# Outer-product decay table, two load queues and zero products at the seam of an attention and a mixture of experts

## The chip, the cores and the metric

The kernel runs on one core of one Trainium2 chip. The metric is device time in microseconds for one execution. Names of engines: TensorE (PE; PEld is its weight load), VectorE (DVE, `nc.vector`, V in the code), ScalarE (ACT, S), GpSimd (POOL, G), SyncE (SP). SP only issues transfers here.

## The reference

A linear attention with a decay per channel feeds a top-1 mixture of eight experts, and that a second dense block. Cut to what matters here:

```python
# attention: B, H, S, D = 2, 8, 768, 48
for t in range(S):
    cur = einsum('bhd,bhe->bhde', u * k[t], v[t])
    y[t] = einsum('bhd,bhde->bhe', r[t], state + cur)
    state = w * state + einsum('bhd,bhe->bhde', k[t], v[t])
# experts: 1536 tokens of 384, 8 experts, d_ff 1024
logits = x @ w_gate
expert = argmax(logits); gate_w = softmax(logits)[expert]
# token i takes the next place in its expert's list
h = relu(x_e @ w1[e]); y = gate_w * (h @ w2[e])
# second block: h = x @ w_in; solu, layer norm; @ w_out
```

`w` lies between 0.85 and 0.95, one number for each channel of each head.

## The kernel before, in words

The attention works in 12 chunks of 128 tokens (`NM = 12`, six for each of the two sequences). A chunk's decay is put into tables: `Pw` holds the powers w^(j-64) and `Qk` their counterparts, for 128 positions j; `rt` is r times `Pw`, `kt` is k times `Qk` (`prelude`), so that `scores(m)` is a product of `kt` and `rt` on TensorE (`sp`), which `mask_scores` masks into `A` on VectorE. `prelude2`, `prelude3` and `weigh` make the term of `u` (`ra`, `vab`) and the decayed keys (`kwb`); `values`, `attend`, `state` and `tokens` make the chunk's outputs `ys` and from them `xp`, the token-major rows with their gate logits.

The front of the kernel loads the decay `wcol`, then for each chunk `rkT` (r and k, channel-major, 512 KB) and `krv` (k, r, v, token-major, 576 KB; chunk 0 in two parts), and `u_sb`, a row of `u` that is read once for each of the 128 partitions, 192 KB. All loads go through SP's queue, in the order of the code. `TB` holds both tables of 130 columns. It is filled by doubling: `square(j)` makes w^(2^j) in `pf`, `invert` the reciprocals, and `extend(j)` doubles the filled part upwards on VectorE and downwards mostly on GpSimd. Chunk 0's `rt` and `kt` are made on VectorE in two halves (`fast=True`), all later ones on GpSimd in whole (128x512). `spare(n, t)` issues n products of a zero tile (`warm`, 512 columns of bf16) whose result nobody reads; 14 stand at the start, 4 ahead of `scores(0)`, 4 ahead of `scores(1)`.

The order on each engine is the order in which the code is written (a manual schedule); tiles get their waits from a framework. TensorE takes its work in that order, so an instruction that waits holds all behind it.

At the end of the attention the routing of the last chunks meets the first expert. For each chunk, `gate1` and `gate2` turn the logits of `xp` into the expert (`oh_all`), the rank of the token in the expert's list (`ranks`, a product on TensorE; `junk` reads it) and the slot; `place(i)` makes the selection matrix `P` on VectorE; `part(i)` makes `xh`, the upper part of the gated row, on ScalarE, and `other(i, xh)` makes `xl`, the rest: on GpSimd for all chunks but the last, on VectorE for chunk 11. `add(i, ...)` multiplies `xh` and `xl` by `P` into the PSUM tile `x0` (`x`, `x0` in the rows), the inputs of expert 0. Their evictions are `xhi` on ScalarE and `xlo` on VectorE; then the experts' products `hps` begin (`mm1`), with weights that ScalarE and VectorE split into `whi` and `wlo`; `hh` and `hl` evict them. `cp` counts the tokens.

Of the kernel before, what the change touches and what calls it, by code (L numbers as in the profile page):

```python
# [8 lines left out]
F32 = mybir.dt.float32  # L9
# [11 lines left out]
C = 128  # L21
# [14 lines left out]
def rwkv_moe_solu_kernel(  # L36
# [106 lines left out]
    def attention(actx):  # L143
# [12 lines left out]
        def load_chunk(m, between=None):  # L156
            a = ld.tile([128, 2, HP, C], F32, tag="rkT", name=f"rkT{m}")
            nc.sync.dma_start(out=a, in_=rkT[:, m])
            if between:
                between()  # L160
            b = ld.tile([128, 3, H, D], F32, tag="krv", name=f"krv{m}")
            chunks[m] = (a, b)
            if m:
                nc.sync.dma_start(out=b, in_=krv[:, m])
            else:
                nc.sync.dma_start(out=b[:, 0:2], in_=krv[:, m, 0:2])
# [7 lines left out]
        nc.sync.dma_start(out=u_sb, in_=u.rearrange("(o h) d -> o h d", o=1).to_broadcast([128, H, D]))  # L174
        load_chunk(1, lambda: nc.sync.dma_start(out=chunks[0][1][:, 2], in_=krv[:, 0, 2]))
# [6 lines left out]
        TB = ac.tile([128, 2, HP, 130], F32, name="TB")  # L182
        TF = TB.rearrange("p s a n -> p (s a) n")
        V.memset(TF[:, :, 64:65], 1.0)
# [8 lines left out]
        spare(WARM, wps)  # L193
        mask = ac.tile([128, 4, C], F32, name="mask")
# [4 lines left out]
        make_identity(nc, ident)  # L199

        acc0 = ac.tile([128, NE], BF16, name="acc0")
        kwb, vab = [], []
        for i in range(3):
            for lst, nm in ((kwb, "kwb"), (vab, "vab")):
                t = ac.tile([128, HP, 2, 64], F32, name=f"{nm}{i}")
                lst.append(t)
        V.memset(ones_b, 1.0)
        V.memset(acc0, 0.0)
        for i in range(3):
            for lst in (vab, kwb):  # L210
                G.memset(lst[i][:, :, :, D:64], 0.0)
# [4 lines left out]
        def square(j):  # L216
            V.tensor_tensor(pf[:, 0, :, j:j + 1], pf[:, 0, :, j - 1:j], pf[:, 0, :, j - 1:j], ALU.mult)

        def invert(a, b):
            V.reciprocal(pf[:, 1, :, a:b], pf[:, 0, :, a:b])  # L220
            G.tensor_copy(pf[:, 2, :, a:b], pf[:, 0, :, a:b])

        def extend(j):
            n = 1 << j
            up, dn = pff[:, 0:2 * HP, j:j + 1], pff[:, HP:3 * HP, j:j + 1]
            k = n if j < 6 else 1
            V.tensor_tensor(TF[:, :, 64 + n:64 + n + k], TF[:, :, 64:64 + k], up.to_broadcast([128, 2 * HP, k]), ALU.mult)
            (V if j == 5 else G).tensor_tensor(
                TF[:, :, 64 - n - k + 1:64 - n + 1], TF[:, :, 64 - k + 1:65], dn.to_broadcast([128, 2 * HP, k]), ALU.mult
            )  # L230
# [993 lines left out]
```

## Time and profile before

| what | us |
|---|---|
| median of 3 runs | 332.63 |
| lowest, highest | 332.2, 334.39 |
| the profiled execution's own time | 333.14 |
| its span, first to last instruction | 331.4 |
| TensorE busy | 315.5 (95%) |
| VectorE busy | 241.7 (73%) |
| ScalarE busy | 186.7 (56%) |
| GpSimd busy | 149.6 (45%) |
| mean granted clock of TensorE | 0.988 |

The span is that of one execution, and the execution's own time holds 1.74 us beside it. A matmul's end is modelled in the trace, so a busy TensorE also holds the time that a product takes to drain. A granted clock of 1.00 is 2.4 GHz, 0.50 is 1.2 GHz. The attention takes the first 77 us, the experts the time to about 205 us, the second block the rest.

### The profile page before, as it was taken

What the parts mean: (1) busy time and instruction counts of PE and PEld (TensorE: products, weight loads), DVE (VectorE), ACT (ScalarE), POOL (GpSimd) and SP (SyncE); (2) the same over time, 40 slices, a digit from 0 to 9 for tenths busy, and PEclk for the clock granted to TensorE, in tenths of its full rate; (3) what the DMA queues carried; (4) which work ended last, traced back from release to release, by engine and by line L of the source; (5) the groups of instructions that cost most, each with busy time, mean ns of one, the idle gap of its engine ahead of it and who ended that gap; (6) DMA issues with size and microseconds to landing.
All of it is one profiled execution on the core that took longest, in us unless ns stands there. A gap on an engine that the chain in (4) does not pass through costs nothing. (4 is left out here: it accounts for less than half of the span.)

```text
span 331.4 us, 7341 instructions
## 1 busy us (share of the span) xinstructions
PE 315.5 (95%) x2736; PEld 290.8 (88%) x2736; DVE 241.7 (73%) x556; ACT 186.7 (56%) x406; POOL 149.6 (45%) x198
## 2 busy tenths in 40 slices
PE   8899989988999999999999999999999999999990
PEld 3688878868999999999999999978999999999990
DVE  7899999957998999898999896258745555434310
ACT  1545646556749796969686867126454433444410
POOL 7889999573523232323232364414254222333321
PEclk9999999997999999999999999999999999999997
DMA  6989999444877999989898913100000000000010
GB/s 202 399 297 292 347 387 401 155 121 107 266 281 247 304 285 292 291 288 274 285 276 293 278 63 50 11 2 1 0 26 25 26 24 24 26 24 24 26 47 24
DMA packets 20395, 56.24 MB, mean 170 GB/s; under 512 B 6594, under 2 KB 9028, under 8 KB 20356
## 3 DMA queue, kind: packets, MB, share of 16 engines
q1 hardware_dynamic: 16916, 47.67, 41.0%
q0 software_dynamic: 3440, 8.06, 10.1%
q8 instruction: 23, 0.38, 0.4%
q14 instruction: 16, 0.13, 0.1%
HBM read 50.56 MB, written 5.16 MB: 168 GB/s over the span
## 5 line engine op out<-in xcount | busy, mean ns | idle before, releaser
L122 DVE TENSOR_TENSOR wlo<-raw,whi 128x768 fp32r<-128x768 f32 x57 | 52.3, 952 | 1.4 <-ACT whi L116 0.9
L804 PE MATMUL yps<-hh,wlo 128*128 128x224 f32 x192 | 52.7, 275 | 0.0
L802 PE MATMUL yps<-hh,whi 128*128 128x224 f32 x192 | 52.7, 275 | 0.0
L803 PE MATMUL yps<-hl,whi 128*128 128x224 f32 x192 | 52.6, 274 | 0.0
L116 ACT ACTIVATE whi<-raw 128x768 fp32r<-128x768 f32 x64 | 50.6, 842 | 0.0
L1044 POOL TENSOR_SCALAR e<-e,nmu 128x1024 f32<-128x1024 f32 x12 | 13.5, 1123 | 62.6 <-DVE nmu L1043 59.5
L1021 DVE TENSOR_REDUCE nm<-h 128x1 f32<-128x1024 f32 (+1 forms) x13 | 14.7, 1140 | 33.0 <-PE h L1010 30.1
L803 PEld LDWEIGHTS yps<-hl,whi 128*128 128x128 f32 x192 | 36.9, 192 | 0.0
L804 PEld LDWEIGHTS yps<-hh,wlo 128*128 128x128 f32 x192 | 36.9, 192 | 0.0
L802 PEld LDWEIGHTS yps<-hh,whi 128*128 128x128 f32 x192 | 36.9, 192 | 0.0
L120 POOL DMA_DIRECT2D wlo<-in_w x7 | 6.9, 986 | 64.6 <-ACT wlo L125 64.6
L1078 PE MATMUL o<-w_hi,shi 128*128 128x384 f32 x96 | 33.1, 345 | 0.0
L1079 PE MATMUL o<-w_lo,shi 128*128 128x384 f32 x96 | 32.2, 335 | 0.0
L1080 PE MATMUL o<-w_hi,slo 128*128 128x384 f32 x96 | 32.2, 335 | 0.0
L94 POOL DMA_INDIRECT xe<-xs,ids x16 | 20.9, 1308 | 20.5 <-PE xt L795 10.7
L816 PE MATMUL hps<-xhi,whi 128*128 128x224 f32 x192 | 28.0, 282 | 0.4 <-issue 0.4
L816 PE MATMUL hps<-xlo,whi 128*128 128x224 f32 x192 | 27.3, 278 | 0.2 <-DVE xlo L798 0.2
L822 ACT ACTIVATE hh<-hps 128x448 fp32r<-128x448 f32 x32 | 17.4, 543 | 17.7 <-PE hps L816 15.7
L816 PE MATMUL hps<-xhi,wlo 128*128 128x224 f32 x192 | 27.2, 278 | 0.0
L816 PEld LDWEIGHTS hps<-xhi,whi 128*128 128x128 f32 x192 | 24.5, 195 | 0.6 <-ACT xg L465 0.5
L816 PEld LDWEIGHTS hps<-xlo,whi 128*128 128x128 f32 x192 | 24.6, 196 | 0.4 <-DVE xlo L798 0.4
L816 PEld LDWEIGHTS hps<-xhi,wlo 128*128 128x128 f32 x192 | 24.7, 196 | 0.0
(185 smaller groups left out, 777.9 us busy)
## 6 DMA issues: line engine op xcount, KB each, us to landing
raw<-in_w SPq DMA_DIRECT2D x32, 768.0 KB
krv<-in_krv SPq DMA_DIRECT2D x11, 576.0 KB
rkT<-in_rkT SPq DMA_DIRECT2D x12, 512.0 KB
w<-in_w_in SPq DMA_DIRECT2D x8, 384.0 KB
w<-in_w_out SPq DMA_DIRECT2D x8, 384.0 KB
wlo<-in_w POOLq DMA_DIRECT2D x7, 384.0 KB
xs<-xg SPq DMA_DIRECT2D x12, 192.0 KB
krv<-in_krv SPq DMA_DIRECT2D x1, 384.0 KB
```

What stands on the lines that cost most here:

```text
L94: nc.gpsimd.indirect_dma_start(out=t[0:n, b, :], out_offset=None, in_=xs[0:rows, :], in_offset=bass.IndirectOffsetOnAxis(ap=ids[0:n, e, c: ...
L116: S.activation(hi, raw, AF.Copy)
L122: V.tensor_tensor(lo, raw, hi.bitcast(F32), ALU.subtract)
L802: T.matmul(ps, w[0][ws], x[0][xsl], start=first, stop=False, skip_group_check=True)
L803: T.matmul(ps, w[0][ws], x[1][xsl], start=False, stop=False, skip_group_check=True)
L804: T.matmul(ps, w[1][ws], x[0][xsl], start=False, stop=last, skip_group_check=True)
L816: T.matmul(ps[:, f], w1s[g][i][:, kk, wf], x[j][:, kk], start=not (i or j or f or kk), stop=j == 1 and kk == KD - 1, skip_group_check=True,)
L822: S.activation(hh, ps, AF.Relu)
L1021: V.tensor_reduce(nms[j], ps, AX.X, ALU.max, negate=True)
L1078: T.matmul(ps, hi[:, f % 4], wo[0][:, f], start=f == 0, stop=False)
L1079: T.matmul(ps, hi[:, f % 4], wo[1][:, f], start=False, stop=False)
L1080: T.matmul(ps, lo[:, f % 4], wo[0][:, f], start=False, stop=f == KF - 1)
```

## The change

The table is built from two short rows. `small_t` holds, for each table, eight fine powers (columns 0 to 7) and sixteen coarse ones in steps of eight (columns 8 to 23); `outer(t, sl)` multiplies them into 128 columns of `TB` for two of the four head pairs. `square` runs six times in a row, one reciprocal covers all powers, `down` fills the coarse row's lower half, three of its four calls on GpSimd. A `V.tensor_copy` of one column per channel goes between. Chunk 0's products follow the outer products half by half. `krv0`'s two parts and `u_sb` are issued from ScalarE's queue, the rest stays on SP's. The front half of `kt1` stays on GpSimd and the back half (`rest`) goes to VectorE behind `mask_scores(0)`. Ahead of `scores(0)` one zero product stands instead of four. At the end of the attention eleven zero products are put in at four places, and `xl` of chunk 10 is made on VectorE behind `P` of chunk 10, no longer on GpSimd.

```diff
-        def load_chunk(m, between=None):
+        def load_chunk(m):
...
-            if m:
+            if m == 0:
+                nc.scalar.dma_start(out=b[:, 0:2], in_=krv[:, m, 0:2])
+            else:
                 nc.sync.dma_start(out=b, in_=krv[:, m])
-            else:
-                nc.sync.dma_start(out=b[:, 0:2], in_=krv[:, m, 0:2])
...
-        nc.sync.dma_start(out=u_sb, in_=u.rearrange("(o h) d -> o h d", o=1).to_broadcast([128, H, D]))
-        load_chunk(1, lambda: nc.sync.dma_start(out=chunks[0][1][:, 2], in_=krv[:, 0, 2]))
+        nc.scalar.dma_start(out=u_sb, in_=u.rearrange("(o h) d -> o h d", o=1).to_broadcast([128, H, D]))
+        nc.scalar.dma_start(out=chunks[0][1][:, 2], in_=krv[:, 0, 2])
+        load_chunk(1)
...
+        small_t = ac.tile([128, 2, HP, 32], F32, name="small_t")
+        SF = small_t.rearrange("p s a n -> p (s a) n")
+        V.memset(SF[:, :, 16:17], 1.0)
+        V.memset(small_t[:, 0, :, 0:1], 1.0)
...
+        def down(eng, j, a, b):
+            eng.tensor_tensor(
+                SF[:, :, a:b], SF[:, :, 17 - (b - a):17], pff[:, HP:3 * HP, j:j + 1].to_broadcast([128, 2 * HP, b - a]),
+                ALU.mult,
+            )
+
+        G.tensor_copy(pf[:, 0, :, 0:1], wcol)
+        make_identity(nc, ident)
+        square(1, low=wcol)
+        for j in range(2, 7):
+            square(j)
+        G.tensor_copy(pf[:, 2, :, 3:7], pf[:, 0, :, 3:7])
+        V.reciprocal(pf[:, 1, :, 0:7], pf[:, 0, :, 0:7])
+        V.tensor_copy(small_t[:, 1, :, 0:1], pf[:, 1, :, 0:1])
+        ups = SF.rearrange("p q (k n) -> p q k n", k=2)
+        for j in range(3):
             n = 1 << j
+            V.tensor_tensor(
+                ups[:, :, :, n:2 * n], ups[:, :, :, 0:n],
+                pff[:, 0:2 * HP, j:j + 4:3].unsqueeze(3).to_broadcast([128, 2 * HP, 2, n]), ALU.mult,
             )
+        down(G, 3, 15, 16)
+        down(G, 4, 13, 15)
+        down(V, 5, 9, 13)
+        down(G, 6, 8, 9)
+        square(7, G)
+
+        def outer(t, sl):
+            V.tensor_tensor(
+                TB[:, t, sl].rearrange("p a (x y) -> p a x y", y=8),
+                small_t[:, t, sl, 8:24].unsqueeze(3).to_broadcast([128, 2, 16, 8]),
+                small_t[:, t, sl, 0:8].unsqueeze(2).to_broadcast([128, 2, 16, 8]), ALU.mult,
+            )
...
+            if m == 0:
+                for sl in (front, back):
+                    outer(0, sl)
+                    outer(1, sl)
+                    weighted(V, rt, tr, Pw, sl)
+                    weighted(V, kt, tk, Qk, sl)
+                return
+            weighted(G, rt, tr, Pw, whole)
+            if m > 1:
+                weighted(G, kt, tk, Qk, whole)
+                return
+            weighted(G, kt, tk, Qk, front)
+            return lambda: weighted(V, kt, tk, Qk, back)
...
-        spare(4, wps)
+        spare(1, wps)
         scores(0)
-        prelude(1)
+        rest = prelude(1)
...
         mask_scores(0)
+        rest()
         together(products)
...
-            if i < NM - 1:
+            if i < NM - 2:
                 G.tensor_tensor(xl, xgs[i], xh.bitcast(F32), ALU.subtract)
...
         m = NM - 1
+        fill = ps_1.tile([128, 512], F32, tag="ra", name="fill")
+        spare(4, fill)
         tokens(m)
...
         scatter(m - 1)
-        los[m - 1] = other(m - 1, his[m - 1])
         store(m - 1)
...
         onehots[m - 1] = place(m - 1)
+        los[m - 1] = other(m - 1, his[m - 1])
         next(steps)
...
-        for i in (m - 1, m):
-            add(i, his)
-            add(i, los)
+        spare(1, fill)
+        add(m - 1, his)
+        add(m - 1, los)
+        spare(3, fill)
+        add(m, his)
+        add(m, los)
...
+        spare(3, fill)
         V.tensor_copy(tot, cp)
```

What stands in a row on the engines. VectorE in the front, before, from the second reciprocal to the front half of chunk 0's products (`TB` is the table, `pf` the powers):

```order
L220 RECIPROCAL pf_107<-pf_107 128x4x4
L227 TENSOR_TENSOR TB_128<-TB_128,pf_107 128x8x8
L217 TENSOR_TENSOR pf_107<-pf_107 128x4
L227 TENSOR_TENSOR TB_128<-TB_128,pf_107 128x8x16
L227 TENSOR_TENSOR TB_128<-TB_128,pf_107 128x8x32
L228 TENSOR_TENSOR TB_128<-TB_128,pf_107 128x8x32
L227 TENSOR_TENSOR TB_128<-TB_128,pf_107 128x8
L262 TENSOR_TENSOR rt0_200<-rkT0_110,TB_128 128x256
L262 TENSOR_TENSOR kt0_199<-rkT0_110,TB_128 128x256
```

Each doubling needs the one before, and the products stand behind the last. The same engine there after the change, from the one reciprocal on (`small_t` holds the two short rows):

```order
L230 RECIPROCAL pf_107<-pf_107 128x4x7
L231 COPY small_t_129<-pf_107 128x4
L235 TENSOR_TENSOR small_t_129<-small_t_129,pf_107 128x16
L235 TENSOR_TENSOR small_t_129<-small_t_129,pf_107 128x16x2
L235 TENSOR_TENSOR small_t_129<-small_t_129,pf_107 128x16x4
L219 TENSOR_TENSOR small_t_129<-small_t_129,pf_107 128x8x4
L246 TENSOR_TENSOR TB_128<-small_t_129 128x256 x2
L269 TENSOR_TENSOR rt0_194<-rkT0_110,TB_128 128x256
L269 TENSOR_TENSOR kt0_193<-rkT0_110,TB_128 128x256
L246 TENSOR_TENSOR TB_128<-small_t_129 128x256 x2
```

The doubling over `TB` has gone, and the products of chunk 0's front half now stand between the outer products of the front and of the back half.

VectorE at the end of the attention, before, from the last gate to chunk 11's `xl`:

```order
L446 RECIPROCAL gate11_1454<-gs11_1430 128x1
L560 TENSOR_SCALAR P0_10_1458<-iota_w_196,t110_1379,rank_all_78 128x224
L450 SCALAR_TENSOR_TENSOR junk11_1460,rank_all_78<-xp11_1389,oh_all_77 128x8
L560 TENSOR_SCALAR P0_11_1462<-iota_w_196,t111_1432,rank_all_78 128x224
L579 SCALAR_TENSOR_TENSOR xl11_1464<-xp11_1389,gate11_1454,xh11_1456 128x384
```

Only chunk 11's `xl` is made there. The same place on VectorE after the change:

```order
L468 RECIPROCAL gate11_1453<-gs11_1431 128x1
L583 TENSOR_SCALAR P0_10_1457<-iota_w_190,t110_1375,rank_all_78 128x224
L602 SCALAR_TENSOR_TENSOR xl10_1459<-xp10_1335,gate10_1400,xh10_1402 128x384
L472 SCALAR_TENSOR_TENSOR junk11_1461,rank_all_78<-xp11_1390,oh_all_77 128x8
L583 TENSOR_SCALAR P0_11_1463<-iota_w_190,t111_1433,rank_all_78 128x224
L602 SCALAR_TENSOR_TENSOR xl11_1465<-xp11_1390,gate11_1453,xh11_1455 128x384
```

`xl10` has come in between `P0_10` and `junk11`, the rank of chunk 11.

TensorE at the end of the attention, before, from the sums of chunk 10 to the counts (`x0` is the first expert's input):

```order
L652 MATMUL x0_1403<-P0_10_1458,xh10_1401 128x224 x3
L652 MATMUL x0_1403<-P0_10_1458,xl10_1446 128x224 x3
L652 MATMUL x0_1403<-P0_11_1462,xh11_1456 128x224 x3
L652 MATMUL x0_1403<-P0_11_1462,xl11_1464 128x224 x3
L696 LDWEIGHTS ones_b_76
L696 MATMUL cp_1498<-acc9_1324,ones_b_76 128x8
```

The sums follow one another. The same place on TensorE after the change, as far as the first of the three zero products ahead of chunk 11's sums:

```order
L192 LDWEIGHTS warm_132
L192 MATMUL fill_1385<-warm_132 128x512
L677 MATMUL x0_1404<-P0_10_1457,xh10_1402 128x224 x3
L677 MATMUL x0_1404<-P0_10_1457,xl10_1459 128x224 x3
L192 LDWEIGHTS warm_132
L192 MATMUL fill_1385<-warm_132 128x512
```

One zero product (`fill`) now stands ahead of chunk 10's sums and three stand between them and chunk 11's; four more stand ahead of `tokens(11)` and three behind the counts.

## Rows read from the trace of the kernel before

**Rows 1.** Page, part 2: TensorE's granted clock in tenths, 40 slices of 8.3 us.
```profile
PEclk9999999997999999999999999999999999999997
```

**Rows 2.** Timeline of TensorE, first expert: start us, us, engine, line, operation, count.
```profile
77.03 1.69 PE L816 MATMUL hps<-xhi,whi 128*128 128x224 f32 x6 [0.38 <-issue]
...
79.80 1.33 PE L816 MATMUL hps<-xlo,whi 128*128 128x224 f32 x6
...
80.96 0.83 PE L816 MATMUL hps<-xhi,whi 128*128 128x224 f32 x6
```

**Rows 3.** Windows of 1 us: busy us by engine, then PEclk, DMA share, GB/s.
```profile
74.00:75.00 1.00, 0.19 (x2) 0.00 (x1) 0.82 (x3) 0.04 (x1) 0.98 (x2) 1.00 0.56 194
...
77.00:78.00 1.00, 0.97 (x4) 0.85 (x5) 0.50 (x2) 1.00 (x3) 0.57 (x1) 0.70 0.55 197
78.00:79.00 1.00, 1.00 (x7) 1.00 (x7) 1.00 (x6) 1.00 (x3) 0.00 (x0) 0.50 0.04 8
```

**Rows 4.** Timeline, end of the attention; in brackets idle time before, and its releaser.
```profile
70.07 1.14 PE L395 MATMUL xp<-sel,ys 112*128 112x104 f32 x8 [0.37 <-ACT ys L346]
...
73.11 0.43 DVE L560 TENSOR_SCALAR P<-iota_w,t,rank_all 128x224 fp32r<-128x224 f32 x1
...
74.25 1.01 POOL L575 TENSOR_TENSOR xl<-xg,xh 128x384 fp32r<-128x384 f32 x1
74.35 1.05 DVE L560 TENSOR_SCALAR P<-iota_w,t,rank_all 128x224 fp32r<-128x224 f32 x1
...
75.31 0.59 PE L652 MATMUL x<-P,xl 128*128 128x224 f32 x3 [1.12 <-POOL xl L575]
75.32 0.61 DVE L579 SCALAR_TENSOR_TENSOR xl<-xp,gate,xh 128x384 fp32r<-128x384 f32 x1
...
76.61 0.85 ACT L691 ACTIVATE xhi<-x 128x224 fp32r<-128x224 f32 x3
...
77.50 0.99 DVE L693 TENSOR_TENSOR xlo<-x,xhi 128x224 fp32r<-128x224 f32 x3 [1.21 <-ACT xhi L691]
...
81.86 0.62 DVE L823 SCALAR_TENSOR_TENSOR hl<-hps,hh 128x448 fp32r<-128x448 f32 x1 [0.66 <-ACT hh L822]
```

**Rows 5.** Windows: ten microseconds of the chunk loop, columns as in rows 3.
```profile
30.00:40.00 10.00, 10.00 (x160) 8.54 (x160) 9.58 (x33) 5.69 (x20) 9.12 (x11) 1.00 0.95 328
```

**Rows 6.** Timeline of the front, columns as in rows 4.
```profile
2.42 1.02 DVE L232 COPY pf<-wcol 128x4 f32<-128x4 f32 x1 [1.05 <-DMA wcol<-in_wd]
...
3.21 0.20 POOL L211 MEMSET kwb<- 128x128 f32 x1
...
3.48 0.37 DVE L217 TENSOR_TENSOR pf<-pf 128x4 f32<-128x4 f32 x2
...
3.88 0.23 DVE L220 RECIPROCAL pf<-pf 128x12 f32<-128x12 f32 x1
...
5.41 1.16 POOL L228 TENSOR_TENSOR TB<-TB,pf 128x64 f32<-128x64 f32 x3
...
5.84 1.18 PEld L191 LDWEIGHTS <-warm 128*128 128x128 bf16 x6 [0.17 <-issue]
...
6.94 0.42 DVE L262 TENSOR_TENSOR rt<-rkT,TB 128x256 f32<-128x256 f32 x1
...
7.96 0.42 DVE L262 TENSOR_TENSOR kt<-rkT,TB 128x256 f32<-128x256 f32 x1
7.97 0.09 POOL L516 MEMSET neg_half<- 128x1 f32 x1
...
10.05 1.18 POOL L262 TENSOR_TENSOR rt<-rkT,TB 128x512 f32<-128x512 f32 x1 [0.89 <-DMA rkT<-in_rkT]
...
12.23 0.57 DVE L269 TENSOR_TENSOR ra<-krv 128x384 f32<-128x384 f32 x1 [0.60 <-DMA krv<-in_krv]
...
12.42 1.16 PE L297 MATMUL sp<-rt,kt 64*128 64x128 f32 x16 [1.59 <-POOL kt L262]
```

**Rows 7.** Windows: half a microsecond of the front, columns as in rows 3.
```profile
6.00:6.50 0.50, 0.50 (x5) 0.20 (x3) 0.50 (x2) 0.00 (x0) 0.50 (x2) 1.00 0.64 145
```

More of the change, by code (lines that the diff above doesn't have):

```diff
@@ L193, in attention @@
         spare(WARM, wps)
+        kwb, vab = [], []
+        for i in range(3):
+            for lst, nm in ((kwb, "kwb"), (vab, "vab")):
+                t = ac.tile([128, HP, 2, 64], F32, name=f"{nm}{i}")
+                lst.append(t)
+                G.memset(t[:, :, :, D:64], 0.0)
         mask = ac.tile([128, 4, C], F32, name="mask")
@@ L219, in invert @@
[L219 to L223, printed above, removed]
-            n = 1 << j
[L225 to L229, printed above, removed]
-            )
@@ L232, in attention, with square @@
-        V.tensor_copy(pf[:, 0, :, 0:1], wcol)
-        square(1)
-        square(2)
-        invert(0, 3)
-        for j in range(3):
-            square(j + 3)
-            extend(j)
-        square(6)
-        invert(3, 7)
-        extend(3)
-        square(7)
-        for j in range(4, 7):
-            extend(j)
-        Pw, Qk = TB[:, 0, :, 0:C], TB[:, 1, :, 1:C + 1]
+        def square(j, eng=V, low=None):
+            low = pf[:, 0, :, j - 1:j] if low is None else low
+            eng.tensor_tensor(pf[:, 0, :, j:j + 1], low, low, ALU.mult)
@@ L246, in attention @@
+        def outer(t, sl):
[4 more added lines that the diff above has]
+            )
+        Pw, Qk = TB[:, 0], TB[:, 1]
         w128 = pf[:, 0, :, 7:8]
@@ L253, in attention, with prelude @@
         rts, kts, avs = {}, {}, {}
-        def prelude(m, fast=False):
+        def prelude(m):
             tr, tk = chunks[m][0][:, 0], chunks[m][0][:, 1]
@@ L259, in prelude, with weighted @@
             kts[m], rts[m] = kt, rt
-            for sl in (slice(0, 2), slice(2, 4)) if fast else (slice(0, 4),):
-                for o, i, t in ((rt, tr, Pw), (kt, tk, Qk)):
-                    (V if fast else G).tensor_tensor(o[:, sl], i[:, sl], t[:, sl], ALU.mult)
+            def weighted(eng, o, i, t, sl):
+                eng.tensor_tensor(o[:, sl], i[:, sl], t[:, sl], ALU.mult)
+            front, back, whole = slice(0, 2), slice(2, 4), slice(0, 4)
+            if m == 0:
[11 more added lines that the diff above has]
+            return lambda: weighted(V, kt, tk, Qk, back)
         def prelude2(m):
@@ L492, in scatter @@
             scattered.append(ins)
-        prelude(0, fast=True)
+        prelude(0)
         gate_on = ac.tile([128, 1], F32, name="gate_on")
```

17 lines of the change are left out of this document (1 added, 16 removed).

## The prediction

> **What bounds the kernel now.** I read the page's slices first, then TensorE's products and the windows where the clock dips, then the chain in front of that place, then the start. The granted clock of TensorE is full except in two slices near a quarter of the span [rows 1]. There the first expert's products begin: the first 18 (three groups of six) take from 77.03 to 80.96, while the six that follow need 0.83 us [rows 2]. The clock is the cause: 0.70, then 0.50 of 2.4 GHz, so from about 77.4 until that faster group it stands at the 1.2 GHz level [rows 3]. Before it fell, TensorE had been busy for only 0.19 us of the microsecond from 74 [rows 3]: it waited 1.12 us for `xl` of chunk 10, which GpSimd wrote until 75.26 [rows 4]. Behind 81 us the experts follow one another on TensorE, so what this place loses the end loses, unless VectorE becomes late. In the chunk loop TensorE is busy 10.00 us of 10 [rows 5], so the loop, too, starts and ends earlier by what its first wait loses: TensorE stands idle 1.59 us before `scores(1)` at 12.42, until GpSimd has made `kt1` [rows 6]. Two places can pay: before 12.42, and from 74 to 81.
>
> **The end of the attention.** Eleven zero products come in there, and each costs 0.20 us (six in 1.18 us) [rows 6].
> The four ahead of `tokens(11)` take 0.80 us where TensorE was idle 0.37 us for `ys` [rows 4], so the chain behind (gate, ranks, place) starts 0.43 us later.
> Against that, `xl` of chunk 10 leaves GpSimd. VectorE's `P` of chunk 11 lasted 1.05 us and ended at 75.40, just after GpSimd's 1.01 us ended at 75.26, where `P` of chunk 10 took 0.43 us [rows 4]; I price it at 0.43 again. The chain then reads: `P` of chunk 10 ends at 73.54 + 0.43 = 73.97; `xl` of chunk 10, now on VectorE, takes 0.61 us as its twin for chunk 11 does [rows 4], until 74.58; the two small operations of the ranks that stood between the rows of `P` take some 0.25 us; `P` of chunk 11 lasts until 75.26 and `xl` of chunk 11 until 75.87. Before, that was 75.32 + 0.61 = 75.93. So the order gains 0.06 us, as good as nothing: what the move gives, the four products take. ScalarE's `xg` and the last adds follow as before, and the evictions `xhi` start at some 76.5 instead of 76.61. The one product and the three between the adds lie where TensorE waits for `xl` and `P`, which covers them; without that wait they would cost 0.8 us.
> The three products behind the counts take 0.60 us and end near 77.1; TensorE would have waited for the third `xhi` until 77.4 anyway (0.85 us from 76.5) [rows 4]. That wait covers them; without it they would cost 0.6 us.
> If the clock stays at 2.4 GHz, the last four of the first six products start at 77.4 and end at 77.9, the next six at 78.8, `xlo` has been ready since 78.4 [rows 4], and the third six end at 79.6. The next group stood at 80.96 [rows 2]: a gain of 1.36 us.
> What is late next is VectorE. It splits weights there almost without a pause, and has little but its idle 0.66 us before `hl` of the first product group [rows 4] and the 0.1 us of the earlier start to give: 0.8 us. TensorE meets it again where the second expert's `xlo` is made. The term is therefore -0.8 to -1.36 us; I take the middle, **-1.1**. Its other bound is 0, if the clock falls all the same.
>
> **The front.** The last `kt0` half ends at 8.38 [rows 6]. The new VectorE chain, from `wcol` at 2.42: six dependent squares at 0.19 us each (two took 0.37), 3.55; a reciprocal of 0.23, 3.8; a copy of four elements, 0.1; four short products, priced as the squares, 4.7; two outer products, priced as the `rt0` row of the same 256 elements, at the 0.34 us that lie between such rows (three of them from 6.94 to 7.96) [rows 6], 5.4; then `rt0` and `kt0` if `rkT0` is there, 6.1; and the same again for the back half, 7.5. That is 0.9 us earlier than 8.38. ScalarE's scaled copies and `QN` follow the table, off the path.
> But `scores(1)` waits for `kt1`, and that for the landing of `rkT1`: GpSimd had been idle 0.89 us when `rkT1` released it at 10.05, and its two products of 1.18 us end at 12.4 [rows 6]. The table alone thus gives nothing here. What gives is the split of `kt1`: GpSimd's second 1.18 us becomes half of one, 0.59 us, and VectorE makes the other half (0.42 us) behind `mask_scores(0)`, about 9.9 to 10.4, beside GpSimd. So -0.59 us at the same landing. Queued behind VectorE's half, which now waits for `rkT1`, are the reduction and `vab0`; `values(0)` needs them only after `scores(1)`, so they hold nobody. The second limit is `krv1`: VectorE waited for it until 12.23, its product takes 0.57 us, and `A` of chunk 1 can follow no sooner than 12.8 [rows 6], while `scores(1)` would now end at 13.0; so little more than -0.6 is to be had unless `krv1`, too, lands earlier. The three zero products that go (0.60 us) lay where TensorE waited for `kt0`.
> The landing itself is the unknown. Ahead of `rkT1` the one queue carries `rkT0`, `krv0`'s first part and `u_sb`; with two queues `rkT1` is second on its own but shares the engines with all of ScalarE's 0.79 MB. The DMA engines moved 145 GB/s where `u_sb`'s broadcast rows run [rows 7], against 328 in the loop [rows 5]. If the second queue brings `u_sb`'s 0.2 MB to that rate, all behind it lands 0.8 us earlier, and the front's best bound is -1.4. If the queues merely share, 0.2 MB more come ahead of `rkT1`, 0.6 us at 328 GB/s, and nothing is left. I take the landing as unchanged, nearer to the row as it is: **-0.6**.
> A rule speaks against the second queue. The Trainium skill, "DMA: Bandwidth & Descriptors", section "Issuing engines are not separate DMA queues", says that transfers of different issuing engines run on the same 16 DMA engines and interleave, so that a second issuer saves only the time of issuing. No run here shows two issuers yet. By it the front gives nothing.
>
> **The sum.** The profiled execution took 333.14 us, 1.74 us more than its span: 333.14 - 1.1 - 0.6 = 331.4. It lay 0.5 us over the median of the runs, 332.63, so against that I forecast **330.9**.
>
> **The rivals.** (1) *The queues only share*: 0 in place of -0.6, 331.5. For it speaks that TensorE's first wait ends with a landing; against it the 145 GB/s, which leave room.
> (2) *The four-element copy is held*. In the trace such a copy lasted 1.02 us and ended at 3.44, just after GpSimd's run of memsets at 3.41 [rows 6]; `P` of chunk 11 shows the same [rows 4]. The new copy is released by the same reciprocal as GpSimd's three short products (1.16 us for three in the old table), behind which its square, iotas and a cast are queued without a wait (from the products' end at 6.57 to 8.06, 1.5 us) [rows 6]. If GpSimd comes first, the copy ends 2.7 us late, near 6.5, the table is whole at 9.3, `A` of chunk 0 ends near 12.2, `vab0` near 13.7, after `scores(1)`, and the loop starts some 0.5 us later than before: 332.0. Against it: the copy is short, and one instruction of GpSimd stands no longer than some 0.4 us.
> The Trainium skill agrees: "GPSIMD Engine Reference", section "1. Specifications", has GpSimd's way into SBUF shared with VectorE, with contention when VectorE works in a 2-port mode; the 1.02 us row bears it out.
> (3) *The clock falls all the same*, behind the zero products: the end term is gone, 332.0. Against it: they put 1.4 us of work where TensorE idled most.
> (4) *Slower: the fall comes ahead of the zero products.* TensorE takes its work in order, and six zero products stand ahead of its last adds and of the first expert. At 1.2 GHz they take 0.40 us each, +1.2, and the six adds 1.33 instead of 0.83 [rows 2], +0.5; with the front's -0.6 and the order's -0.1 that is +1.0, 333.6. It decides by when the clock falls: before about 75, rather than at 77.4. For it: the chain now starts 0.43 us later, so TensorE still idles between the adds; against it: four products fill the time right before.
>
> **How the numbers follow.** Both places pay: 0.50. Rival 1: 0.18; rival 2: 0.15; rival 3: 0.08; rival 4: 0.06; the rest is unnamed. Low end: both best bounds, -1.4 and -1.36, from 332.63, 329.9, less 0.5 for the spread of the runs: 329.4. High end: rival 2 or 3 with the same spread, 332.5. One per cent, about what a measurement of this kernel can tell from no change, is 3.3 us; both best bounds make 2.8. So faster by more 0.08, within 0.89, slower 0.03.
>
> **What would show it.** The first expert's products in groups of 0.83 us from the second group on, and a clock of 1.00 from 74 to 82; `P` of chunk 11 at 0.4 us; `kt1` in two halves that overlap, `scores(1)` near 11.8; VectorE's copy at 0.1 us. The forecast fails if `rkT1` lands elsewhere than near 10 us, if TensorE's idle time near 10 us lowers the clock in the chunk loop, or if VectorE eats the gain between 81 and 95 us.

## The result, and the profile after

The changed kernel takes 336.35 us (median of four runs, 336.06 to 337.2), the kernel before 332.89 in the same comparison (four runs, 332.2 to 334.39): a ratio of 1.0111, 95% interval 1.0079 to 1.0143. It is slower by about 1%, where 330.9 was forecast. The profiled execution took 336.44 us with a span of 334.7, against 333.14 and 331.4: 3.3 us more.

Two marks divide the span: the start of `scores(11)`, the last chunk's, and the first expert's fourth group of six products, the first that ran at full speed before [rows 2]. From the start to `scores(11)` the kernel before takes 62.28 us and the changed one 65.42 (+3.14). From there to the fourth group it is 18.68 against 16.91 (-1.77), and from the fourth group to the end 250.44 against 252.37 (+1.93). So the front or the loop loses, the end of the attention wins as it was meant to, and something behind it takes that win back. These are two single profiles; how far such marks move from one profile to the next is said under the table of experiments.

The page's slices of the granted clock show the first two of these. The dip near a quarter of the span [rows 1] is gone, and a new one stands in the second slice:

```profile
PEclk9799999999999999999999999999999999999997
```

**The front.** VectorE's rows of the changed kernel (start, duration, operation, and in brackets the idle time ahead and what ended it):

```profile
3.62 0.17 DVE L216 TENSOR_TENSOR pf<-wcol 128x4 f32<-128x4 f32 x1 [2.21 <-DMA wcol<-in_wd]
...
5.26 0.17 DVE L231 COPY small_t<-pf 128x4 f32<-128x4 f32 x1
...
6.36 0.76 DVE L246 TENSOR_TENSOR TB<-small_t 128x256 f32<-128x256 f32 x2
7.97 0.42 DVE L269 TENSOR_TENSOR rt<-rkT,TB 128x256 f32<-128x256 f32 x1 [0.84 <-DMA rkT<-in_rkT]
```

`wcol` comes 1.2 us later than the 2.42 of [rows 6], and when the front half of the table is ready, VectorE waits again, for `rkT0`; before, its `rt0` row of 6.94 waited for no landing. `rkT0` is issued at 1.23 and is there 6.7 us later; on one queue (b_split and a_nosplit below) it lands 4.2 us after its issue. GpSimd, behind that:

```profile
10.67 0.19 POOL L540 COPY held<-gate_on 128x1 f32<-128x1 f32 x1 [3.08 <-DVE gate_on L521]
10.81 1.27 POOL L269 TENSOR_TENSOR rt<-rkT,TB 128x512 f32<-128x512 f32 x1
```

This is one way by which a late front reaches the loop (the other is VectorE's own queue, see a_spare below): in both kernels GpSimd's work on chunk 1 stands behind `held`, a copy of `gate_on`, and VectorE writes `gate_on` behind chunk 0's products, here at 10.54. `rkT1` holds nobody: it landed near 9.8 us (8.1 us after its issue at 1.70). Before, the copy was done by 9.2 and it was the landing of `rkT1` that released GpSimd, at 10.05 [rows 6]. TensorE, in the same stretch:

```profile
1.31 6.05 PE L192 MATMUL wps<-warm 128*128 128x512 bf16 x15 [1.31 <-DVE warm L187]
8.78 0.71 PE L319 MATMUL sp<-rt,kt 64*128 64x128 f32 x8 [1.42 <-DVE kt L269]
10.12 1.23 PE L319 MATMUL sp<-rt,kt 64*128 64x128 f32 x8 [0.62 <-DVE kt L269]
...
12.19 1.69 PE L192 MATMUL wps<-warm 128*128 128x512 bf16 x4
13.81 1.16 PE L319 MATMUL sp<-rt,kt 64*128 64x128 f32 x16
```

The two halves of `scores(0)` are eight products of the same shape each, but 0.71 us becomes 1.23, and four zero products take 1.69. The second half and what follows run at the lower level of the clock, by the window's granted clock (columns: busy time and instructions of PE, PEld, DVE, ACT and POOL, then clock, DMA share, GB/s):

```profile
10.00:15.00 5.00, 4.88 (x33) 3.29 (x34) 4.68 (x9) 1.65 (x7) 4.04 (x5) 0.66 1.05 396
```

`scores(1)` starts at 13.81 instead of 12.42 [rows 6]. From `scores(2)` to `scores(11)` the loop takes 46.22 us (19.20 to 65.42) against 45.06 before, and there GpSimd's products have become slower than the 1.18 us of [rows 6] (grouped by line, 14 to 70 us; total, mean ns):

```profile
L269 POOL TENSOR_TENSOR rt<-rkT,TB 128x512 f32<-128x512 f32 x10 | 13.1, 1306 | 0.0
L269 POOL TENSOR_TENSOR kt<-rkT,TB 128x512 f32<-128x512 f32 x10 | 13.0, 1301 | 0.0
```

**The end of the attention.** The first expert's groups stand 0.67 to 0.74 us apart from the first on, where [rows 2] has groups of 1.3 to 1.7 us. The first of them comes no sooner behind `scores(11)` than before (14.83 us against 14.75); the whole gain lies between the groups:

```profile
80.25 0.90 PE L845 MATMUL hps<-xhi,whi 128*128 128x224 f32 x6
80.99 0.83 PE L845 MATMUL hps<-xhi,wlo 128*128 128x224 f32 x6
81.66 0.83 PE L845 MATMUL hps<-xlo,whi 128*128 128x224 f32 x6
82.33 0.83 PE L845 MATMUL hps<-xhi,whi 128*128 128x224 f32 x6
```

**Behind it.** VectorE's rows from 87 us: three of them, each 0.2 to 0.6 us long elsewhere, take about 3 us and end together near 91.18:

```profile
87.57 0.35 DVE L910 TENSOR_SCALAR da<-w 128x384 int32<-128x384 int32 x1
87.84 3.34 DVE L761 TENSOR_SCALAR cnt<-tot 128x8 f32<-128x8 f32 x1
87.96 3.22 DVE L912 SCALAR_TENSOR_TENSOR da<-w,da 128x384 int32<-128x384 int32 x1
88.44 2.75 DVE L763 TENSOR_SCALAR cnt<-tot 128x8 f32<-128x8 f32 x1
91.24 0.56 DVE L914 CUSTOM_DVE_ANT_0 da<-w,da 128x768 uint16<-128x768 uint16 x1
```

At the same time GpSimd makes the descriptors of the second expert's gather and then eight memsets without a pause; the last ends at 91.15:

```profile
85.36 1.82 POOL L94 DMA_INDIRECT xe<-xs,ids  x1 [5.03 <-DMA ids<-idx]
87.49 1.02 POOL L94 DMA_INDIRECT xe<-xs,ids  x1 [0.31 <-issue]
88.52 0.49 POOL L952 MEMSET yThi<- 128x448 f32 x1
...
90.85 0.30 POOL L952 MEMSET yTlo<- 128x224 f32 x1
```

TensorE pays for it ten microseconds later (weight load row):

```profile
100.71 0.74 PEld L845 LDWEIGHTS hps<-xlo,whi 128*128 128x128 f32 x6 [1.73 <-DVE xlo L827]
```

In the kernel before, the same memsets ran from 84.42 to 87.06, and only one row, `da` at 86.28 with 1.00 us instead of 0.35, was held, until just behind their end. They moved because the gather waits for `ids`, not for TensorE: it starts 4.05 us later (85.36 against 81.31), while TensorE's fourth group and VectorE's decoding come only some 1.3 us later. Of the 4.05 us, 2.78 are the later scatter of the ids, and 1.27 the longer way from the scatter to the gather (6.00 us against 4.73). The second part isn't the change's doing: b_split below, which leaves this place as it was, has 6.00 us too, and a long hold.

### The profile page after: what moved, and what is told of

The parts are those of the page before. It is cut to its first block, busy times and chain, and to the rows that moved or that the text cites. A ratio compares the mean times of both kernels' runs of the same rounds, so it can differ in the third digit from the quotient of the medians.

```text
span 334.7 us, 7358 instructions
## 1 busy us (share of the span) xinstructions
PE 317.3 (95%) x2744; PEld 290.7 (87%) x2744; DVE 246.6 (74%) x557; ACT 186.8 (56%) x406; POOL 149.1 (45%) x195
## 5 line engine op out<-in xcount | busy, mean ns | idle before, releaser
L845 PE MATMUL hps<-xhi,whi 128*128 128x224 f32 x192 | 27.1, 277 | 0.1
L845 PEld LDWEIGHTS hps<-xhi,wlo 128*128 128x128 f32 x192 | 24.0, 192 | 0.0
```

The costliest lines, as they stand in the source:

```text
L845: T.matmul(ps[:, f], w1s[g][i][:, kk, wf], x[j][:, kk], start=not (i or j or f or kk), stop=j == 1 and kk == KD - 1, skip_group_check=True,)
```

## The experiments

**Theory.** Three costs that the prediction had left out make the loss: the second queue delays the loads on which the front waits; GpSimd's products are slower with rows of 128 elements in the table; and GpSimd's memsets hold VectorE. **Rivals:** the clock in the front is the whole of the front's loss; VectorE has too much work behind 82 us. Every kernel's ratio is to the kernel before, run beside it.

| kernel | ratio, 95% interval | `scores(11)` | to the fourth group | to the end |
|---|---|---|---|---|
| before | 1 | 62.28 | 18.68 | 250.44 |
| changed | 1.0111 (1.0079 to 1.0143) | 65.42 | 16.91 | 252.37 |
| a_oneq | 1.0045 (1.0025 to 1.0065) | 63.08 | 17.46 | 252.46 |
| a_spare | 1.0097 (1.0071 to 1.0123) | 65.22 | 17.43 | 252.45 |
| a_tb130 | 1.0079 (1.0049 to 1.0109) | 64.46 | 17.26 | 252.28 |
| a_mem | 1.0079 (1.0049 to 1.0110) | 65.39 | 17.47 | 251.24 |
| b_tail | 0.9996 (0.9967 to 1.0024) | 61.57 | 17.07 | 252.46 |
| b_tailclear | 0.9936 (0.9913 to 0.9959) | 61.86 | 17.34 | 250.00 |
| b_split | 0.9996 (0.9970 to 1.0021) | 61.94 | 18.25 | 252.31 |
| a_best1 | 0.9958 (0.9936 to 0.9981) | 62.02 | 17.39 | 249.89 |
| b_clear | 0.9970 (0.9938 to 1.0003) | 62.10 | 20.45 | 249.95 |
| b_fillclear | 0.9941 (0.9921 to 0.9962) | 61.60 | 17.59 | 250.01 |
| a_wcol | 1.0164 (1.0126 to 1.0201) | 66.34 | 16.42 | 252.44 |
| a_nosplit | 0.9927 (0.9900 to 0.9954) | 62.11 | 17.42 | 250.07 |
| a_gateq | 1.0154 (1.0126 to 1.0183) | 69.47 | 17.29 | 252.34 |
| a_pad | one run, 335.98 us | 64.35 | 17.49 | 252.46 |

The three columns on the right are the three parts of each profiled span. They vary from one execution to the next, too: over the five traces whose front is that of the kernel before (before, b_tail, b_tailclear, b_clear, b_fillclear), `scores(1)` starts between 11.70 and 12.42 and `scores(11)` between 61.57 and 62.28.

**One queue (a_oneq).**

```diff
-            nc.scalar.dma_start(out=b[:, 0:2], in_=krv[:, m, 0:2])   # m == 0
+            nc.sync.dma_start(out=b[:, 0:2], in_=krv[:, m, 0:2])
-nc.scalar.dma_start(out=u_sb, ...)
-nc.scalar.dma_start(out=chunks[0][1][:, 2], in_=krv[:, 0, 2])
-load_chunk(1)
+nc.sync.dma_start(out=u_sb, ...)
+load_chunk(1, lambda: nc.sync.dma_start(out=chunks[0][1][:, 2], in_=krv[:, 0, 2]))
```

> The changed kernel with all of the front's loads back on SyncE's queue, in the order of the kernel before. If the second queue is what made the front late: wcol lands near 2.4 us instead of 3.62, rkT0 before 7 instead of 7.97, scores(0) starts about 1.1 us earlier, scores(1) near 12.7 instead of 13.81; the rest of the loop and the end keep their losses, so 335.0 us against 336.35 for the changed kernel. If the queue costs nothing on the path and the clock near 10 us is the whole of the front's loss (the rival): wcol may land early, but scores(1) stays at 13.4 or later, 336.2 us.

Measured: `wcol` is there again at 2.50 (VectorE's rows), `rt0` starts at 6.26 without a wait, `scores(0)` at 7.07, `scores(1)` at 11.22, earlier than in any trace of the old front; the clock stays at 1.00 in the windows to 68 us.

```profile
2.50 0.40 DVE L217 TENSOR_TENSOR pf<-wcol 128x4 f32<-128x4 f32 x1 [1.09 <-DMA wcol<-in_wd]
...
6.26 0.42 DVE L270 TENSOR_TENSOR rt<-rkT,TB 128x256 f32<-128x256 f32 x1
```

The ratio falls from 1.0111 to 1.0045, 0.66% or 2.2 us; `scores(11)` comes 2.34 us sooner. The second queue is the largest of the costs found. That its loads hinder each other by sharing the DMA engines fits `rkT0`'s 6.7 us against 4.2, but no run shows how they do it.

**Three zero products back ahead of `scores(0)` (a_spare).**

```diff
-        spare(1, wps)
+        spare(4, wps)
         scores(0)
```

> The changed kernel with the three zero products put back ahead of scores(0). If TensorE's idle 1.42 us before scores(0) is what lowers the clock from 10 to 15 us: the granted clock of that window goes from 0.66 to about 0.9 or more, the back half of scores(0), the four transposes and the four zero products ahead of scores(1) take 1.5 us less, scores(1) starts near 12.9, 335.2 us. If the clock falls for the later idle time of 0.62 us, or falls all the same (the rival): the clock stays near 0.66 and the time at 336.3 us.

The clock does stay up, as expected (window of this kernel):

```profile
10.00:15.00 5.00, 4.16 (x42) 2.96 (x44) 4.93 (x8) 1.56 (x7) 4.43 (x5) 1.00 1.06 400
```

and `scores(1)` starts at 12.73 instead of 13.81. But `scores(2)` comes at 18.95 against 19.20, `scores(11)` at 65.22 against 65.42, and the ratio, 1.0097, is not to be told from 1.0111. TensorE's rows of a_spare:

```profile
1.31 5.94 PE L192 MATMUL wps<-warm 128*128 128x512 bf16 x18 [1.31 <-DVE warm L187]
8.69 0.71 PE L319 MATMUL sp<-rt,kt 64*128 64x128 f32 x8 [1.44 <-DVE kt L269]
...
14.17 0.62 PE L339 MATMUL yp<-ident,vab 128*112 128x128 f32 x4 [0.27 <-DVE vab L307]
...
18.40 0.62 PE L339 MATMUL yp<-ident,vab 128*112 128x128 f32 x4 [1.08 <-DVE vab L307]
```

The three products didn't shorten the idle time that was under suspicion: it is 1.44 us, as long as the 1.42 without them, because the 18 zero products took no longer than the 15 of the changed kernel. So the idle time by itself doesn't lower the clock. The five traces with the changed front and one zero product (changed, a_tb130, a_mem, a_pad, a_wcol) all show 0.66 or 0.67 in this window, this one shows 1.00; that the three products make the difference is likely, but it rests on one trace. The price is clear: behind `scores(1)` TensorE waits here for `vab0` and `vab1`, the end of VectorE's chain, which the clock of TensorE doesn't touch, and GpSimd's first product of chunk 1 starts at 10.72 here and at 10.81 there. So the clock is not the front's loss.

**Rows of 130 elements (a_tb130), and with both tables at column 0 (a_pad).**

```diff
-        TB = ac.tile([128, 2, HP, C], F32, name="TB")
+        TB = ac.tile([128, 2, HP, 130], F32, name="TB")
-        Pw, Qk = TB[:, 0], TB[:, 1]
+        Pw, Qk = TB[:, 0, :, 0:C], TB[:, 1, :, 1:C + 1]     # a_tb130
+        Pw, Qk = TB[:, 0, :, 0:C], TB[:, 1, :, 0:C]         # a_pad
```

> The changed kernel with the tables of powers in rows of 130 elements, the keys' table starting at column 1, as in the kernel before; everything else as changed. If the narrower rows made GpSimd's products slow: its rt and kt rows in the loop go back from 1.30 to 1.18 us, the loop loses 1.1 us less between scores(2) and scores(11), 335.2 us. If they are slow for another reason (the place of other tiles, VectorE's work beside them): the rows stay at 1.30 us and the time at 336.3 us.

> The changed kernel with the tables in rows of 130 elements, both starting at column 0. If the length of the rows is what counts: rt and kt on GpSimd at 1.18 to 1.22 us. If the column at which the keys' table starts counts: kt stays at 1.30 us and rt with it.

GpSimd's rows in a_pad (those of a_tb130 read 1221 and 1217):

```profile
L269 POOL TENSOR_TENSOR rt<-rkT,TB 128x512 f32<-128x512 f32 x10 | 12.2, 1222 | 0.0
L269 POOL TENSOR_TENSOR kt<-rkT,TB 128x512 f32<-128x512 f32 x10 | 12.2, 1215 | 0.0
```

From `scores(2)` to `scores(11)` both take 45.26 us, as against 46.22 of the changed kernel; every kernel with rows of 130 needs 45.06 to 45.46, every one with rows of 128 46.22 to 46.88. So the length of the rows counts and the column doesn't: 1.0 us. One rival is left: a longer table also moves the tiles behind it, by 64 bytes in each partition, and no run separates this from the length. The single ratio, 1.0079, agrees, but alone would not tell a_tb130 from the changed kernel's 1.0111.

**The memsets ahead of the gather: four of them (a_mem), or all eight (b_tailclear, b_clear and others below).** Four were moved in a_mem, not eight as its expectation says; the other four belong to the next expert and are issued right behind the gather.

```diff
+        clear(0)              # the four memsets of yT of expert 1
+        clear(1)              # the four of expert 2; not in a_mem
         xraw = load_xe(1, 0, 2)
...
```

> The changed kernel with the eight memsets of the output rows put ahead of the second expert's gather on GpSimd, so that they run while it waits for the ids. If these memsets and the gather hold VectorE from 87.9 to 91.2: the two rows of cnt go from 3.34 and 2.76 to 0.17 us, da from 3.22 to 0.56, TensorE's wait of 1.5 us for xlo goes, and with it 1.9 us: 334.4 us. If VectorE is late there because it has too much to do, as the prediction's bound had it (the rival): the rows get short, but TensorE waits as before, 336.0 us or more.

The held row shrinks with the memsets that are left, and ends again with the last of them (VectorE, then GpSimd, of a_mem):

```profile
88.37 2.06 DVE L761 TENSOR_SCALAR cnt<-tot 128x8 f32<-128x8 f32 x1
88.49 1.94 DVE L912 SCALAR_TENSOR_TENSOR da<-w,da 128x384 int32<-128x384 int32 x1
```

```profile
88.03 1.01 POOL L94 DMA_INDIRECT xe<-xs,ids  x1 [0.31 <-issue]
89.05 0.49 POOL L943 MEMSET yThi<- 128x448 f32 x1
...
90.10 0.30 POOL L943 MEMSET yTlo<- 128x224 f32 x1
```

The last part of the span falls from 252.37 to 251.24 us, and TensorE's longest wait for `xlo` from 1.5 to 0.9 us; the ratio, 1.0079, is not to be told from 1.0111. The theory's size was half right because the edit was half of it.

**The end of the attention alone, on the kernel before (b_tail), and with the eight memsets ahead (b_tailclear).** b_tail is the diff of the change from `other` on and nothing else.

> The kernel before with the change's end of the attention alone: the eleven zero products, and xl of chunk 10 on VectorE. If the prediction's end term is right: no clock fall near 78, the fourth group of six products (80.96 us) 1.4 to 1.9 us earlier, and 0.8 to 1.4 us off the time of the kernel before. If the gain is given back because the second expert's gather, and the memsets behind it on GpSimd, come later against TensorE's work and hold VectorE's integer and count rows for some 3 us instead of 0.6 (my theory): the products are as early, but the time is within 0.4 us of the kernel before, and rows of cnt or da of 2 to 3.3 us stand between 85 and 90.

> The same, with the eight memsets of the output rows put ahead of the second expert's gather. If they are what holds VectorE: the held rows shrink to what the gather itself takes (1.0 us or less), and the time is 1.0 to 1.8 us below the kernel before. If the gain is lost elsewhere behind 82 us (VectorE's own work, the landing of the ids, the gather): no more than 0.5 us below it.

b_tail shows both halves of my theory. The fourth group comes 17.07 us after `scores(11)` instead of 18.68, no window is below 1.00 to 100 us, and the time is the kernel before's: 0.9996. VectorE and GpSimd in b_tail:

```profile
84.22 3.34 DVE L738 TENSOR_SCALAR cnt<-tot 128x8 f32<-128x8 f32 x1
84.33 3.22 DVE L889 SCALAR_TENSOR_TENSOR da<-w,da 128x384 int32<-128x384 int32 x1
```

```profile
84.89 0.48 POOL L929 MEMSET yThi<- 128x448 f32 x1
...
87.22 0.30 POOL L929 MEMSET yTlo<- 128x224 f32 x1
```

With the memsets ahead, from 77.19 to 80.84, the same rows are short, TensorE is busy 10.00 us of each 10 from 80 to 100, and 0.9936 is 2.1 us below the kernel before:

```profile
84.78 0.17 DVE L738 TENSOR_SCALAR cnt<-tot 128x8 f32<-128x8 f32 x1
84.90 0.56 DVE L889 SCALAR_TENSOR_TENSOR da<-w,da 128x384 int32<-128x384 int32 x1
```

The rival falls: VectorE has the same work in both, and keeps up once it isn't held. The gather by itself holds nothing: its second part runs from 84.38 to 85.45, right beside these short rows.

**The memsets alone (b_clear).**

> The kernel before with nothing but the eight memsets put ahead of the second expert's gather. In its profile they held VectorE for 0.64 us only, so by that row alone it should be within 0.3 us of the kernel before. If other executions of the kernel before have the long hold too (the profile of the kernel with the split alone had one of 3.0 us), it is 0.5 to 1.5 us faster, and the tail's own gain is the rest of the 2.1 us.

0.9970, with an interval that just takes in 1; the second expectation is the nearer one. The last part is 249.95 us, half a microsecond below the kernel before's profile and 2.4 below the traces with the long hold. That profile's short hold was thus one of two that occur: b_split has a long one. The zero products' own gain is what lies between b_clear and b_tailclear, 0.34% or 1.1 us; the two intervals overlap. The single executions tell more: of b_clear's twelve, four took 330.08 to 330.62 us at a mean granted clock of 0.992 to 0.994, as b_tailclear's eight did (329.85 to 330.99, 0.992 to 0.995), and four, the profiled one among them, 333.78 to 334.25 at 0.979 to 0.983. So without the zero products the clock's loss differs from one execution to the next, and what they buy is that it stays small in all.

**Zero products without the move of `xl` (b_fillclear).** The diff of b_tailclear without the three places of `xl`.

> The kernel before with the eleven zero products and the memsets ahead of the gather, but with xl of chunk 10 on GpSimd and in its old place. By the prediction's step the zero products keep the clock up and the move gives back what the four ahead of the last tokens take (0.43 us): no clock fall, 0.3 to 0.5 us slower than with the move, so about 1.7 us below the kernel before. If the clock falls all the same while TensorE waits for that xl (the rival): the first groups take 1.3 to 1.7 us again, and it is less than 1.2 us below.

0.9941 against 0.9936: no difference. The clock stays up, and the expected loss of 0.3 to 0.5 us isn't seen. In this execution `P` of chunk 11 took 0.53 us beside GpSimd, not the 1.05 of [rows 4].

**Half of the second `kt` on VectorE, alone on the kernel before (b_split).**

```diff
-        prelude(1)
+        prelude(1, late=late)      # G: rt whole, kt[:, 0:2]
         mask_scores(0)
+        late.pop()()               # V: kt[:, 2:4] = tk * Qk
```

> The kernel before with half of the second chunk's k on VectorE alone. If the prediction's term is right: scores(1) 0.6 us earlier at the same landing of rkT1, scores(11) and the end 0.5 to 0.6 us earlier. If the chunk loop takes it back because GpSimd's chain, not scores(1), sets the pace (the rival): scores(1) near 11.8, scores(2) within 0.2 us of 17.2, the time within 0.2 us of the kernel before.

0.9996. `scores(1)` starts at 11.66, but the traces with the unsplit front have 11.70 to 12.42. The two engines stand in each other's way: VectorE's half runs beside GpSimd's `rt1` (9.61 to 10.79) and then beside GpSimd's half (VectorE, then GpSimd):

```profile
9.92 1.15 DVE L265 TENSOR_TENSOR kt<-rkT,TB 128x256 f32<-128x256 f32 x1
```

```profile
10.75 0.86 POOL L264 TENSOR_TENSOR kt<-rkT,TB 128x256 f32<-128x256 f32 x1
```

instead of 0.42 and 0.59 us. From GpSimd's first product of chunk 1 at 9.61 to `scores(1)` it is 2.05 us, against 2.37 unsplit [rows 6]: 0.3 us, which the loop doesn't pass on (5.13 us from `scores(3)` to `scores(4)` here, 4.96 before).

**The three costs taken out together (a_best1), and that without the split (a_nosplit).** One queue, rows of 130, the eight memsets ahead; in a_nosplit `kt1` is GpSimd's alone.

> The changed kernel with the three suspected costs taken out together: the front's loads on one queue, the tables in rows of 130, the eight memsets ahead of the gather. If the queue, GpSimd's slower products and the held VectorE are the whole loss: scores(11) near 61.9, the fourth group of six near 79.6, no held row over 1.1 us, and 2.0 to 2.6 us below the kernel before. If they are not (the rival): within 1 us of the kernel before.

> One queue, tables in rows of 130 and memsets ahead of the gather, as in the run with the three costs taken out, but with the whole kt of the second chunk on GpSimd: of the change's front only the outer products are left. If the split is worth its 0.59 us: 0.4 to 0.6 us slower than that run, so some 0.9 us below the kernel before. If VectorE's half and GpSimd's hinder each other so that the split gives nothing (0.94 us for VectorE's half in that run, 0.42 expected): scores(1) within 0.3 us of 11.5, and 1.2 to 2.0 us below the kernel before.

The marks of a_best1 came as expected (62.02, 79.41, no held row); the ratio, 0.9958, is 1.4 us below the kernel before, less than the 2.0 to 2.6 expected, though its span is 2.1 below. a_nosplit gives 0.9927, 2.4 us below; `scores(1)` at 12.12 is later than my 11.5. The split gains nothing in either comparison. Beside a_nosplit, a_best1 starts `scores(1)` 0.93 us earlier, `scores(2)` 0.34 and `scores(11)` 0.09: between the first two TensorE waits twice for `vab`, which stands behind the half of `kt1` in VectorE's queue (TensorE's rows of a_best1; in a_nosplit neither waits):

```profile
12.63 0.62 PE L340 MATMUL yp<-ident,vab 128*112 128x128 f32 x4 [0.28 <-DVE vab L308]
...
16.02 0.62 PE L340 MATMUL yp<-ident,vab 128*112 128x128 f32 x4 [0.24 <-DVE vab L308]
```

The kernel a_nosplit is the fastest measured, 1.8% below the changed one (0.9927 / 1.0111), though not to be told from b_tailclear: the outer products, by themselves, leave the time as it was.

**What a second queue does (a_wcol, a_gateq).**

```diff
-nc.sync.dma_start(out=wcol, in_=wd)                   # a_wcol
+nc.scalar.dma_start(out=wcol, in_=wd)                 # a_wcol: first on ScalarE's queue
+V.tensor_copy(chunks[0][1][:, 0, 0, 0:1], wcol[:, 0]) # a_gateq: ScalarE's three loads wait for it
```

> The changed kernel with wcol's load moved ahead of the others on ScalarE's queue, so that no large load is issued before or beside it. If the late wcol (3.62 us) alone makes the front late: it lands near 2.5, scores(0) starts near 7.2, the clock stays up, and the time falls by 2 us against the changed kernel, to 0.45 per cent over the kernel before. If rkT0, which shares the engines with 0.6 MB of the other queue, sets the pace as well (my theory): scores(0) no sooner than 8.2, and no more than 0.7 us is won.

> The changed kernel with ScalarE's three loads held until wcol has landed (one more small copy on VectorE, 0.2 us). If wcol's lateness is the cost of the second queue: wcol lands near 2.5, scores(0) starts near 7.4, the clock stays up, and the time is that of the kernel with one queue, 0.3 to 0.6 per cent over the kernel before. If the large loads of two queues hinder each other as well (the rival): rkT0 lands after 7.2, scores(0) starts at 8.2 or later, 0.8 per cent or more over it.

Both came out slower than the changed kernel. a_gateq's rival had that sign, but not its reason: `rkT0` is in time there. In a_wcol the small load, though first in its queue, landed at 4.97 (VectorE's row), while `rkT0` was issued beside it at 0.80 on the other queue, against what its expectation says; `scores(0)` starts at 9.21, and `rt0` doesn't wait for `rkT0`:

```profile
4.97 0.17 DVE L216 TENSOR_TENSOR pf<-wcol 128x4 f32<-128x4 f32 x1 [3.56 <-DMA wcol<-in_wd]
```

In a_gateq `wcol` lands in time and `scores(0)` starts at 7.07, as that theory said, but now ScalarE's loads, issued from 2.63 behind SyncE's, come late: `krv0`, `u_sb`, and last the part of `krv0` that `vab0` needs (VectorE):

```profile
9.11 0.57 DVE L291 TENSOR_TENSOR ra<-krv 128x384 f32<-128x384 f32 x1 [0.76 <-DMA krv<-in_krv]
...
10.81 0.57 DVE L293 TENSOR_TENSOR ra<-ra,u_sb 128x384 f32<-128x384 f32 x1 [1.07 <-DMA u_sb<-in_u]
...
15.42 0.56 DVE L307 TENSOR_TENSOR vab<-krv,ra 128x384 f32<-128x384 f32 x1 [1.81 <-DMA krv<-in_krv]
```

`scores(2)` then starts at 22.65. So it is neither `wcol` alone nor `rkT0` alone: one queue's order is the order in which the front needs its loads, and with two queues some load that is needed early runs beside or behind one that isn't.

## Why the prediction was wrong, point by point

- **"The clock fall ... avoided"**: right. The mark of the end term, from `scores(11)` to the fourth group, is 16.4 to 17.6 us in the thirteen traces with zero products and 18.25 to 20.45 in the three without. The term of -0.8 to -1.36 was -1.77 in this profile: the working gave each group 0.83 us, a row that holds the end of its last product too, and the groups stand 0.67 to 0.74 us apart. That the order of the operations would gain as good as nothing was right as well (14.83 us to the first group, 14.75 before).
- **"What is late next is VectorE"**: the engine and the place were right (`xlo` of the second expert), the reason and the size weren't. I took VectorE's own work as the limit and left it 0.8 us of slack. What is late there is VectorE held by GpSimd, and that takes 2.4 us of the end: 252.3 to 252.5 us behind the fourth group with the long hold, 249.9 to 250.1 without. The kernel before's profile lost some 0.4 of it, the changed one all. This step, a gain of 1.1 us, gave 0: b_tail 0.9996. The row that announced it stood in the trace of before (`da`, 1.00 us, ending with the memsets), and I had used that very mechanism elsewhere, in rival 2.
- **"I take the landing as unchanged"**: the step that failed most. The landing itself came as taken, near 9.8 us; what was wrong is that it sets the start of chunk 1. I asked only when `rkT1` would land, worked the table's chain "from `wcol` at 2.42", and took -1.4 to 0 as the bounds; that `wcol` and `rkT0` could come later beside the new queue was in no term. They did (3.62 and 7.97 us), VectorE's chain with them, and through `gate_on` GpSimd's first product of chunk 1, 10.81 instead of 10.05. The second queue cost 2.2 us (a_oneq), and the term of -0.6 counts nothing for it. Rival 1 had the mechanism, but with 0 as its worst. The Trainium skill's rule, "DMA: Bandwidth & Descriptors", section "Issuing engines are not separate DMA queues" (transfers interleave whoever issues them), agrees with `rkT0`'s 6.7 us from issue to use instead of 4.2; its conclusion, that a second issuer saves the issuing time alone, is too kind here: `wcol` came at 3.62 and 4.97 instead of 2.42 to 2.50.
- **The table's chain, "7.5"**: with `wcol` in time its back half ends at 8.36 (a_oneq), as late as before. The outer products stand 0.34 us apart as priced, but the short operations took longer: from 2.50 to the first outer product at 5.59 it is 3.1 us, where I had some 2.3.
- **"So -0.59 us at the same landing"**: not found (b_split 0.9996; a_nosplit is, if anything, faster than a_best1). Running half on VectorE beside GpSimd assumed each at its own speed; 0.42 became 1.15 and 0.59 became 0.86. And of the reduction and `vab0`, queued behind VectorE's half, the prediction says that "they hold nobody": with the new front TensorE waited 0.28 us for `vab0` and 0.24 for `vab1` (a_best1), 0.56 for `vab1` in the changed kernel.
- **Unpriced: GpSimd's products.** No term asks what the new table's narrower rows do to them. With these rows 1.18 us becomes 1.30, and the loop takes 1.0 us more.
- **"The three zero products that go ... lay where TensorE waited"**: true in time, since the idle time is the same with and without them, but without them the clock fell. The forecast's own condition of failure (idle time near 10 us lowers the clock) came about in so far; it cost 1.1 us at `scores(1)` and 0.2 at `scores(11)`.
- **Rival 2** (the four-element copy held): no. It took 0.17 us at 5.26, ahead of GpSimd's products (5.38). But the ground given against it, that one instruction of GpSimd is short, doesn't carry: the hold behind 82 us lasted until a whole run of memsets was over.

The sum as measured: second queue +2.2, narrow rows +1.0, tail -1.8, hold +1.9 make +3.3, the difference of the spans. The first term is a difference of ratios, the others come from single profiles, and the +1.9 is against the one profile of before, whose hold was short; how much of the hold the change itself adds is not shown.

## What to carry to other kernels

Loads on one queue are a schedule: before moving some to a second, list for every load that is needed early what will now run beside it, the small ones first. When a seam is tightened on one engine, look at which engine's fixed bursts (memsets, descriptors) now meet another's work; such a burst belongs where no other engine has work that it holds, and here moving eight memsets made a gain of nothing into one of 2.1 us. A step that is split over two engines should be priced with both running, and with what then stands behind it in the second engine's queue. A single profile is one draw: here `scores(1)` moved by 0.7 us between traces of the same front.

## What the runs showed of the hardware

- VectorE rows of 0.17 and 0.56 us lasted until a whole run of GpSimd's instructions had ended, not one of them: 3.34 us across one gather and eight memsets, 2.06 across one and four, none when the memsets lay elsewhere, with the gather still beside the rows (b_tailclear). The Trainium skill, "SBUF — State Buffer", section "Who interferes with whom", has the shared port as a lock that is held "for the whole instruction"; here, with GpSimd's memsets issued without a pause, the lock as VectorE sees it lasted for the run. Its product rows `wlo` beside the same memsets were not held (in b_tailclear two take 1.82 us from 79.04, as in the other traces).
- GpSimd's 128x512 product takes 1.30 us with the table's rows at 128 elements and 1.22 with 130 (1.27 to 1.29 and 1.19 to 1.20 with one load queue, a_oneq and a_best1), the work as it was. Why isn't known, nor whether the length of the rows or the place of the tiles behind the table does it.
- TensorE's clock fell to the lower level near 10 us after idle times of 1.42 and 0.62 us around 0.71 us of work (0.66 in the window from 10 to 15 us). With three zero products more ahead of the same idle times, 1.44 and 0.62 us, it stayed at 1.00 (a_spare, one trace).
- Not settled: why the way from the scatter to the gather takes 4.73 us in one trace and up to 6.72 in another (6.00 in the changed kernel and in b_split, 6.72 in a_oneq). It decides where the memsets fall.
